# A linear-attention and MLP kernel whose five written-out queues are ordered anew with refitted transfer times

## The chip, the cores and the metric

One core of a Trainium2 chip runs one launch of the whole program. The metric is device time in microseconds (us), as the median of repeated runs. The engines are TensorE (PE, with its weight loads as PEld), VectorE (DVE), ScalarE (ACT), GpSimd (POOL) and SyncE (SP, whose queue issues the transfers).

## The reference

The input is a block of 2048 rows of 512 numbers. Two layers A and B follow each other, and both are applied twice with the same weights.

```python
def _A_ref(x, wqkv, w_phi, wo):
    q, k, v = ((x @ wqkv).reshape(B, S, 3, H, Dh)...)        # H = 32, Dh = 16
    phi_q = concat([softmax(q @ w_phi), softmax(-(q @ w_phi))])  # per head; the same for k
    kv, z = phi_k^T v, sum(phi_k)                            # over all 2048 rows
    o = (phi_q kv) / (phi_q z + 1e-6)
    return o.reshape(B, S, D) @ wo

def _B_ref(x, w1, w2):
    return relu(x @ w1) @ w2                                 # 512 -> 1792 -> 512

x = A_x
x = x + _A_ref(layernorm(x), A_wqkv, A_w_phi, A_wo)
x = x + _B_ref(layernorm(x), B_w1, B_w2)
x = x + _A_ref(layernorm(x), A_wqkv, A_w_phi, A_wo)
x = x + _B_ref(layernorm(x), B_w1, B_w2)
```

## The kernel before

The rows are worked on in 16 chunks of 128, and the MLP in 8 groups of 256. Each f32 operand of a product is held as the sum of two f16 numbers, high and low, and three products (high by high, high by low, low by high) stand for one. ACT makes most high parts by copying, and POOL or DVE subtract to get the low parts.

*Layer A.* Each chunk `x` is normalised (`n_a`), turned by a transposing DMA or at the start by PE (`xT`), and projected to `pk`, `pv` and `pq`. The feature map makes exponentials (`e_k`, `e_q`), a factor (`fm_k`, `fm_q`) and the products `p_k`, `p_q`. A product with `minus` gives the low part of `v` from the same bank after ACT has copied the high part (line 795). `kv` and `kvn` collect phi_k^T v over the rows, `pn` multiplies them with the transposed `pT`; a division gives `o`, which is split in high and low parts (`n_o`), turned to `oT` and projected by `pw`. `qs` is the copy of `pq` that goes to memory (`q_dram`) and comes back as `ql`. `xt_dram` keeps a chunk's `xT` for the later query projection.

*Layer B.* `n_b` is turned to `yT`. For most groups the hidden product (lines 1391 to 1500, `hidden_by_seven`) multiplies by seven half-size products in place of eight. It needs sums of weight blocks, made at the start by POOL and ACT (`sums`, `sums_h`, `sums_l`), kept in `s_dram`, and loaded again as `s` for each step (`fetch_sums`, line 1391, 512 KB into one of three buffers). ACT copies the intermediate results to `sn` (line 1446), and DVE adds them back (lines 1452, 1457). The output product by seven is line 1608, the plain one line 1549.

*The order.* Nothing runs in program order of this file. Each operation is registered with `add(engine, work, ...)` in a `Plan`: 4681 tasks, 1513 on PE, 972 on DVE, 1071 on ACT, 618 on POOL and 506 on SP. `ORDER` holds one string for each of the five queues. Read from left to right, a digit says how many of the tasks left over in this engine's list are skipped before the next is taken (`Z` adds 61). So the strings alone fix what each engine does after what. `order()` then replays the queues with the planner's model times and hands out the tasks by their modelled starts; with the queues fixed, its times decide only in which sequence the instructions of different engines are written down. `landing()` is the model's price of a transfer: time from issue to landing, and the time the queue takes for each. A transposing transfer is `turn`; a task with `work > 1.5` that isn't `turn` is another class, and all the rest the third. The issue itself is priced in `add`, for a transposing load in `transposed`: 1.3 us below 512 KB, else 1.85. [...]

The engines take their queues strictly in sequence. A step that stands too early makes everything behind it in its queue wait.

The function that the diff touches is `Plan.landing` (line 177), called by `Plan.order`, beside the table `ORDER`.

Of the kernel before, what the change touches and what calls it, by code (L numbers as in the profile page):

```python
# [54 lines left out]
DIGITS = "0123456789abcdefghijklmnopqrstuvwxyzABCDEFGHIJKLMNOPQRSTUVWXYZ"  # L55
ORDER = {
    PE:
        "000033222242210032000770204413339122603847310830209001180032710013140020331403160D516201xx12v04314031012"
        "555520eeee10cc0bbn0aaaaiiaaaa01070605600302011190011040000a058000200500344070101405046103050332700150055"
        "71783070351544403300111133311000004700000000000000000007090000d00b00f00i00j00000000000000000000001111133"  # L60
        "33333333304444444410222333133302222222222000000001112222201001106009000000000300090001111122000000000002"
        "222220110001030000000000000007090g000d00h000j0l00000j000000000000000000000000222222222111333333333334445"
        "55550444444444444445556666666607706666770605566677788888aaa099900700550446605550444444033333312222222222"
        "22222222222222201122201110110000000000011111444444444447777777060555555088880777770055999900700040001111"
        "111060000006b000000000000000001111111111010ps0r202000liij00g00e0ddeedd0c0f10dff0cdcc00a00807700904444445"
        "540330011311003330223307770667700aa0027005556605aaaaaaaaaaaaaaaaaaabbbccccccccdddee0000a0990807005514033"
        "30222011111111110400500000j000000g0000000000e000000000j0000000000000A0C0000000000000000000C000C000000000"
        "000000v000000000000000000000000l00000000000000000y000y000000000000000000z000000000000q0000000r0000000000"
        "0000000o00000000000000000000000v0000000000000000000000c000s000s0000000000000000000000e00000000000000e000"
        "0000000000v00w00000000000000000y000000v000000000000r000000000000000000000000h000000000000000000000000000"  # L70
        "00000000000000000000000000000000000000000000000000000000000000000000000000000000000000000000000000000000"
        "000000000000000000000000000000000000000000000000000000010",
    DVE:
        "330430210000e222011036000020dd0302203a35d33b602f230c100e0YdX0g00Te04f4Oe4g660Id5f004403902h20f1h1g10000e"
        "j0idg7063f04033028k222222220441312110343llm34j33h33333c320122121006k01i410200abe0q0d7n004100o03mf02j0400"
        "01800d4100003630136051150664650514099317011300aa108000131321521300060240661666058408070450020051411c3b32"
        "924302002063522322001113110223302004410209107025e01c12a2010203132152131811050718817569189841004090016011"
        "10211130226176625582756827360c00aahh0g000220b11107011063341509544225452332403000252031403514180701194406"
        "680881065160146002211062520331601410h4g0001232117011060045141010000000330520120000010k0100g00000b0a09102"
        "0c1b4002000030g3f311cx016u15s111003t3s032p6252LL4090HO80M706JZaZa05Z825467053513077Z4ZC1300Z00Zw044V1Zr7"  # L80
        "0201e120Zs21Zq10800d0ZjZP1ZO10912100ZG115501315041020de1001Zv102h3Zqg0004g422200292Zb00224002520303f2200"
        "22a002300024222817029200224007262110g2g2200201j02h3015022220b0228102a59010622002200211023100522220020102"
        "20021102000201023000342320022002000221022000010011010",
    ACT:
        "31201104220030005c5ba099fm088c306053cc10jj2902md2cj1003mZq320j141Zj0m2kZf0j1500k3k0j26gn2m5j1136312k3Mj4"
        "1222ll4010m10130h3021102301cc041gg310002801cc002060201bj2216312c1110k8jjd80g0f69da080d7c460307010aaa0301"
        "c0b0fa020c650400d40309gg18020b03600080740200100020850033494104501011403a3480262303201110141023500820a053"
        "032000020431012057115c53022201131020220251131303231010350243242021010142832204b4590302533333343350030004"
        "182b716191071018111222015261553544512362605599909808807cc0ccf00ef0ie00f0e2420a1d10b709250968073433a39383"
        "393570250a1912100510383067096106608533504321003044239a003305200550002041700122100605210643021004033020g0"  # L90
        "0e010524010504008d0770999051f05300322030014255016ecb101990u80607p067605v56060ep583m406I05G950D70Q677Zp6M"
        "6ZmL7777Zh805608043Zo44ZY032Zj04Zh4ZQ400011011040ZEf302ZQ52ZO4036311ZZjf33ZE110302224000ZZ31005042300030"
        "32200l605520052033135100f3ZG30141022010Ze22Zs0115044011102330006055246004030004140332501027011302B001044"
        "00014140220160j501360240306021g4021100222103020105042370501302070024400524401004003320030220030220030201"
        "03022103302040302200303321403020130220403305103000000",
    POOL:
        "10002540570095006800960A0z96019600607005908a00809e00710c91118100101106252201b01f4e8000044403005201ck20a1"
        "c10ac09fbb910000143032131201100000022e017215100071630221111162100200103022010304444300131323101110001111"
        "104470082466053022110046004200312201413444430003400000001ccc1300077b706686056051433300130220302222200022"
        "4050002200000100000000302104030000066000001000000aa010002d00009cc0k0juYua01U8100203W10Zo0T1000Zid203Zn30"  # L100
        "23322b01Zd100011105Zw000061000010g3302021302221d11044012201T5111Y101121000242010222141121441730200003000"
        "l13110002222a0022111d1114133001114070004411002422002221110044440333312100000000000002333220110000000100",
    SP:
        "200010100214060809Badf119eg02s8127nc5e065Cd1223322235b90a1220704i1g1jg112e31b3002708d0fe30e21e00g2q51na2"
        "D3320e11g013100A8f002573b3b4537580c42a4120171159565a6hb4aa358l6124133884t486Bc3fh77055454b9597255520w0c7"
        "73272a6067ac8cq5a46371644418136371259d052c10aa112b3a448a0902bcJb72946772692556651823o124907731w5314300r1"
        "p2668o4841367436D1qd3110d235h0moqw7011009d1v0g709a00ex2E40g06K4811b12807aHg8Q9la70826Q2Z15233k72721456j1"
        "535Q51430205h51043044504d122200403063529244302218504070226452432205040044440330113022110010",
}


# [32 lines left out]
class Plan:  # L144
# [1936 lines left out]
```

## Time and profile before

| what | value |
|---|---|
| median of 3 runs | 964.04 us (963.81 to 964.42) |
| profiled execution | 963.83 us, span 962.1 us |
| PE busy | 947.4 us, 98% |
| DVE, ACT, POOL busy | 694.8, 573.6, 647.5 us |
| memory traffic | 144 GB/s over the span, read 108.30 MB, written 30.15 MB |
| granted clock of PE | top tenth in all 40 slices |

Busy time is what an engine's instructions take in the profile; the ends of products on PE are modelled, so a busy PE isn't always at its peak. A wait is put down to the engine or transfer that released it last. The profile comes from one execution, and the span is 1.73 us shorter than that execution's device time.

### The profile page before, as it was taken

The numbers are of one execution on the slowest core, as the hardware profiler recorded it, in microseconds if no ns is written. First come the engines' busy times: TensorE is split into PE (matmuls) and PEld (weight loads), VectorE is DVE, ScalarE is ACT, GpSimd is POOL, SyncE is SP. The second block draws the span as 40 slices with busy tenths as digits, with TensorE's granted clock in tenths as the row PEclk, the third lists the DMA queues.
The fourth block names the chain that finished last, engine by engine and source line by source line (L and its number), as shares of the span: only waits on it lengthen the run. The fifth ranks groups of instructions, "written<-read, shape, count | busy, mean of one in ns | idle before, by whom it ended". The sixth has DMA issues, their size and how long they took to land.

```text
span 962.1 us, 23668 instructions
## 1 busy us (share of the span) xinstructions
PE 947.4 (98%) x9372; PEld 659.7 (69%) x9372; DVE 694.8 (72%) x1408; ACT 573.6 (60%) x1121; POOL 647.5 (67%) x634
## 2 busy tenths in 40 slices
PE   8999999999999999999999999999999999999997
PEld 5544555666665766566677775566666889888997
DVE  6899978856876877766566678987886575665455
ACT  7999978654554636454375555465555565555553
POOL 2699877778685857555376647267578888777644
PEclk9999999999999999999999999999999999999999
DMA  9387858499869697788649864599999786886541
GB/s 334 90 223 197 194 157 224 95 197 217 206 156 233 164 268 158 175 224 214 155 155 253 254 189 112 199 248 228 222 221 252 184 186 170 188 169 172 134 139 66
DMA packets 251807, 183.38 MB, mean 191 GB/s; under 512 B 180656, under 2 KB 188080, under 8 KB 251696
## 3 DMA queue, kind: packets, MB, share of 16 engines
q1 hardware_dynamic: 251696, 181.87, 74.3%
q8 instruction: 73, 1.20, 0.5%
q14 instruction: 38, 0.31, 0.1%
HBM read 108.30 MB, written 30.15 MB: 144 GB/s over the span
## 4 chain that ended last, share of the span: by engine, by line
PE 91%; DMA 2%; ACT 2%; POOL 2%; DVE 1%; issue 1%; SPq 0%; DVEq 0%; POOLq 0%; ACTq 0%
PE ph L1433 23%; PE py L1549 14%; PE py L1608 12%; PE pw L650 8%; PE pk L650 8%; PE pv L650 8%; PE pq L650 8%; PE ph L1513 3%; PE pn L1019 2%; PE kv L816 1%; DMA s<-s_dram 1%; DMA st_k<-in_A_wqkv_dram 1%; DMA wk_h<-n_u 1%; POOL sums L1289 0%; POOL p_q L734 0%
## 5 line engine op out<-in xcount | busy, mean ns | idle before, releaser
L1549 PE MATMUL py<-w,h 128*128 128x512 f16 x690 | 174.2, 379 | 0.0
L1433 PEld LDWEIGHTS <-s 128*128 128x128 f16 x2352 | 151.3, 98 | 28.3 <-DMA s<-s_dram 2.2
L1446 ACT ACTIVATE sn<-ph 128x128 f32<-128x128 f32 x294 | 80.6, 274 | 146.3 <-PE ph L1433 143.2
L650 PEld LDWEIGHTS <-xT 128*128 128x128 f16 x900 | 86.8, 98 | 99.1 <-DMA xT<-n_a 1.4
L1433 PEld LDWEIGHTS <-w 128*128 128x128 f16 x1764 | 111.0, 98 | 15.0 <-DMA wk_h<-n_u 1.4
L1433 PE MATMUL ph<-yT,s 128*128 128x128 f16 x1176 | 97.6, 219 | 1.1 <-DVE ph L1452 1.1
L1433 PE MATMUL ph<-yT,w 128*128 128x128 f16 x1176 | 97.6, 219 | 0.0
L1452 DVE TENSOR_TENSOR ph<-ph,sn 128x128 f32<-128x128 f32 x98 | 29.3, 299 | 92.3 <-PE ph L1433 48.5
L1549 PEld LDWEIGHTS <-h 128*128 128x128 f16 x690 | 61.4, 98 | 49.2
L734 POOL TENSOR_TENSOR p_q<-e_q,p_q 128x1024 f16<-128x1024 f32 x32 | 71.4, 2230 | 21.0 <-ACT p_q L730 21.0
L723 POOL TENSOR_TENSOR e_q<-e_q,fm_q 128x1024 f32<-128x1024 f32 x32 | 62.5, 1957 | 33.8 <-ACT fm_q L719 33.5
L734 POOL TENSOR_TENSOR p_k<-e_k,p_k 128x1024 f16<-128x1024 f32 x30 | 68.7, 2288 | 20.6 <-ACT p_k L730 20.5
L650 PE MATMUL pw<-wo_h,oT 128*128 128x512 f16 x256 | 81.4, 379 | 0.2 <-ACT qs L886 0.2
L650 PE MATMUL pk<-wk_h,xT 128*128 128x512 f16 x256 | 81.3, 379 | 0.0
L650 PE MATMUL pv<-wv_h,xT 128*128 128x512 f16 x256 | 81.2, 379 | 0.0
L723 POOL TENSOR_TENSOR e_k<-e_k,fm_k 128x1024 f32<-128x1024 f32 x30 | 59.5, 1983 | 28.7 <-ACT fm_k L719 27.7
L650 PEld LDWEIGHTS <-oT 128*128 128x128 f16 x384 | 37.0, 98 | 41.4 <-issue 1.0
L1457 DVE TENSOR_TENSOR ph<-ph,sn 128x256 f32<-128x256 f32 x98 | 41.9, 427 | 31.1 <-PE ph L1433 30.6
L1608 PEld LDWEIGHTS <-h 128*128 128x128 f16 x648 | 59.1, 98 | 6.4
L1229 POOL TENSOR_TENSOR w<-r 128x256 f32<-128x256 f32 x41 | 31.4, 766 | 40.0 <-ACT r L1225 40.0
L650 PE MATMUL pq<-wq_h,xq 128*128 128x512 f16 x168 | 56.6, 379 | 0.1
L1608 PE MATMUL py<-w,h 128*128 128x256 f16 x324 | 53.0, 273 | 0.0
(279 smaller groups left out, 2419.4 us busy)
## 6 DMA issues: line engine op xcount, KB each, us to landing
s<-s_dram SPq DMA_DIRECT2D x98, 512.0 KB, 4.4
q_dram<-qs SPq DMA_DIRECT2D x28, 256.0 KB, 3.8
ql<-q_dram SPq DMA_DIRECT2D x28, 256.0 KB, 3.7
u<-t_dram SPq DMA_DIRECT2D x13, 512.0 KB, 4.5
xt_dram<-xT SPq DMA_DIRECT2D x21, 256.0 KB, 4.2
xq<-xt_dram SPq DMA_DIRECT2D x21, 256.0 KB, 3.9
xe<-in_A_x_dram SPq DMA_DIRECT2D x16, 256.0 KB, 4.4
x<-in_A_x_dram SPq DMA_DIRECT2D x16, 256.0 KB, 4.2
```

The lines of the kernel that those rows point to most:

```text
L650: nc.tensor.matmul(pm.ap, xT.ap[:, a, k, :], W.ap[b][:, k, :], start=(k == 0 and i == 0), stop=(k == KC - 1 and i == 2))
L723: (nc.vector if fast else nc.gpsimd).tensor_tensor(e3, e3, sm.unsqueeze(2).to_broadcast([P, 2 * n, DH]), op=ALU.mult)
L734: (nc.vector if fast else nc.gpsimd).tensor_sub(part16(1, cols), part16(1, cols, ef), part16(0, cols))
L1019: nc.tensor.matmul(at()[:, g, :], pT.ap[:, a, 4 * i + g, :], r[b].ap[:, 4 * i + g, :], start=(j == 0), stop=(j == 2))
L1229: nc.gpsimd.tensor_sub(rf.ap[:, :2, :], r.ap.rearrange("p (a b) -> p a b", a=4)[:, ::3, :], block(1).unsqueeze(1).to_broadcast([P, 2, P]))
L1433: nc.tensor.matmul(at(r), weight_of(i, b, kk, s, summed), rows_of(y, i, a, kk), start=(first and kk == 0 and n == 0), stop=(kk == 1 and n ...
L1446: nc.scalar.activation(saved(i), at(2), AF.Copy)
L1452: add(DVE, 0.27, lambda: nc.vector.tensor_tensor(at(3), at(1), saved(2), op=ALU.add), reads=[(ph, 1), (sn, 2)], writes=[(ph, 3)], boost=10 ...
L1457: add(DVE, 0.40, lambda: nc.vector.tensor_tensor(wide(ph), wide(ph), wide(sn), op=ALU.add), reads=[(sn, 0), (sn, 1)], writes=[(ph, 0), (ph ...
L1513: nc.tensor.matmul(at()[:, j, cs.start * P:cs.stop * P], W1.at(b, k, slice(f * P, (f + 1) * P)), yT.ap[:, cs, a, k, :], stop=(k == KC - 1 ...
L1549: nc.tensor.matmul(py.ap, h[a].ap.rearrange("p j t -> p (j t)")[:, cols], W2.at(b, fs[j], slice(0, D)), start=(begins and j == k == 0), st ...
L1608: nc.tensor.matmul(py.ap[:, 256 * r:256 * r + 256], left[a], right[b], start=(s == 0 and r == 0 and k == 0), stop=(last and k == 2), skip_ ...
```

## The change

The strings of all five queues are replaced, and the three prices in `landing` are changed. No operation is added or removed, and no buffer changes its size or number. In numbers for common sizes: a 256 KB transfer 2.62 us before and 2.91 after; a 512 KB one 3.65 and 4.03; a transposing load of 256 KB 3.16 and 3.11, of 512 KB 4.33 and 4.61. Decoded, 845 of PE's 1513 tasks keep their place; on DVE 366 of 972, on ACT 361 of 1071, on POOL 253 of 618 and on SP 74 of 506. The mean shift is 0.88 places on PE, 1.32 on DVE, 1.40 on ACT, 1.20 on POOL and 3.90 on SP; the longest are 34 places on PE, 30 on DVE, 38 on ACT, 12 on POOL and 66 on SP. Some of the moves: the square of `st_q` on ACT from place 20 to 17; the `pv` product with `minus` on PE near 127 us from 102 to 111; `pn` products near 732 us from 1026 to 1033 and from 1030 to 1041; a `pw` near 830 us from 1244 to 1235; an `n_o` on ACT from 890 to 873 and a high `p_q` from 907 to 869; two stores to `xt_dram` near 432 us on SP from 246 to 208 and from 241 to 261.

The first line of each string, before and after, and the prices:

```diff
--- before.py
+++ after.py
     PE:
-        "000033222242210032000770204413339122603847310830209001180032710013140020331403160D516201xx12v04314031012"
...
+        "000032222422210032000770204413339122053847300840209002910032701013140304015041710D51620y1xx3040152030036"
...
     DVE:
-        "330430210000e222011036000020dd0302203a35d33b602f230c100e0YdX0g00Te04f4Oe4g660Id5f004403902h20f1h1g10000e"
...
+        "33043302100f3331221812211001di03b022c2022c42290112c1bg1Z110Y0hc00Te0g44e4Mg660Id500d440a302h20f1h1g100g0"
...
     ACT:
-        "31201104220030005c5ba099fm088c306053cc10jj2902md2cj1003mZq320j141Zj0m2kZf0j1500k3k0j26gn2m5j1136312k3Mj4"
...
+        "31011004220001105bb5aa09nf2087b0h1553cl0029h30dl2kc1003Zr30kk214Zk00l2Zgk3j6204k0k0ji722mm511U7331m23kb1"
...
     POOL:
-        "10002540570095006800960A0z96019600607005908a00809e00710c91118100101106252201b01f4e8000044403005201ck20a1"
...
+        "11030854006058009600960A09y6019600607060908a00809e007109b11181001011062522d010a1e94800910405340030c0fb11"
...
     SP:
-        "200010100214060809Badf119eg02s8127nc5e065Cd1223322235b90a1220704i1g1jg112e31b3002708d0fe30e21e00g2q51na2"
...
+        "200010002004069d020d8yea39920s07863014M556923482371b3b6b23m20070131g41g41410830c78f0k03fe0220eit2r101030"
...
@@ -177,10 +177,10 @@
     def landing(self, t):
 
         if t.turn:
-            return 2.0 + t.kb / 220, t.kb / 230
+            return 1.6 + t.kb / 170, t.kb / 193
         if t.work > 1.5:
-            return 4.8, 2.4
-        return 1.6 + t.kb / 250, t.kb / 385
+            return 4.4, 2.5
+        return 1.8 + t.kb / 230, t.kb / 306
 
     def add(self, engine, work, fn, reads=(), writes=(), makes=(), lock=False, kb=0, turn=False, boost=0,
             after=(), slack=None):
```

## Rows read from the trace of the kernel before

**Rows 1.** The page: busy time by engine; granted clock of TensorE in 40 slices.

```profile
PE 947.4 (98%) x9372; PEld 659.7 (69%) x9372; DVE 694.8 (72%) x1408; ACT 573.6 (60%) x1121; POOL 647.5 (67%) x634
...
PEclk9999999999999999999999999999999999999999
```

**Rows 2.** Stretches: length, busy PE PEld DVE ACT POOL, clock, DMA share, GB/s.

```profile
0.00:30.00 30.00, 25.45 (x161) 18.37 (x162) 21.19 (x56) 22.89 (x37) 8.28 (x24) 1.00 0.80 290
...
930.00:960.00 30.00, 27.16 (x333) 24.52 (x330) 16.77 (x32) 12.20 (x30) 14.21 (x21) 1.00 0.19 66
...
sum 962.10, PE 947.41 PEld 659.70 DVE 694.81 ACT 573.58 POOL 647.46; mean PE 28.71 PEld 19.99 DVE 21.05 ACT 17.38 POOL 19.62
```

**Rows 3.** Waits of PE: total us, times, longest us.

```profile
PE wt_k L1731 <- DMA st_k<-in_A_wqkv_dram: 2.0, 2, 1.5
PE ph L1433 <- DMA s<-s_dram: 1.9, 2, 1.2
```

**Rows 4.** Timeline of PE, single lines: start us, us, line, operation, idle before.

```profile
23.11 1.04 PE L1731 MATMUL wt_q<-ident,st_q 128*128 128x128 f32 x8
...
127.83 0.39 PE L795 MATMUL pv<-v,minus 128*128 128x512 f16 x1 [0.69 <-ACT v L791]
...
189.91 0.38 PE L650 MATMUL pw<-wo_h,oT 128*128 128x512 f16 x1 [0.25 <-ACT qs L886]
190.12 0.38 PE L650 MATMUL pw<-wo_l,oT 128*128 128x512 f16 x1
...
385.84 0.84 PE L1433 MATMUL ph<-wq_h,s 128*128 128x128 f16 x12 [0.73 <-DMA s<-s_dram]
...
438.09 0.84 PE L1433 MATMUL ph<-wq_l,s 128*128 128x128 f16 x12 [1.18 <-DMA s<-s_dram]
...
732.07 0.51 PE L1433 MATMUL ph<-wk_h,w 128*128 128x128 f16 x6 [1.26 <-DMA wk_h<-n_u]
...
834.70 0.38 PE L650 MATMUL pw<-wo_h,oT 128*128 128x512 f16 x1
```

**Rows 5.** Timeline of ACT, single lines.

```profile
21.22 0.58 ACT L1736 COPY wT_q<-wt_q 128x512 f32<-128x512 f32 x1
21.68 1.92 ACT L387 ACTIVATE wq_l<-st_q 128x2048 bf16<-128x2048 f32 x1
...
127.18 0.60 ACT L791 ACTIVATE v<-pv 128x512 f16<-128x512 f32 x1
...
188.22 1.15 ACT L1279 ACTIVATE sums_h<-sums,s_w 128x1024 f16<-128x1024 f32 x1 [3.18 <-POOL sums L1289]
...
827.11 0.63 ACT L564 ACTIVATE n_o<-o 128x512 f16<-128x512 f32 x1 [1.34 <-issue]
...
832.25 0.28 ACT L1446 ACTIVATE sn<-ph 128x128 f32<-128x128 f32 x1 [0.34 <-PE ph L1433]
```

**Rows 6.** Timeline of SP's queue, single lines.

```profile
378.05 3.27 SPq L578 DMA_TRANSPOSE pT<-p_q  x1
...
432.08 0.46 SPq L772 DMA_DIRECT2D xt_dram<-xT  x1
...
721.96 3.74 SPq L578 DMA_TRANSPOSE pT<-p_q  x1
...
829.00 1.24 SPq L578 DMA_TRANSPOSE oT<-n_o  x1
```

**Rows 7.** Pieces of the chain that ended last: start us, us, what.

```profile
381.41 4.38 DMA s<-s_dram
431.67 6.37 DMA s<-s_dram
...
726.42 5.60 DMA wk_h<-n_u
```

**Rows 8.** DMA issues: transfer, times, KB, median us from issue to landing.

```profile
s<-s_dram SPq DMA_DIRECT2D x98, 512.0 KB, 4.4
...
oT<-n_o SPq DMA_TRANSPOSE x28, 3.7
```

More of the change, by code (lines that the diff above doesn't have):

```diff
@@ L68 @@
[L68 to L70 removed]
+        "000032222422210032000770204413339122053847300840209002910032701013140304015041710D51620y1xx3040152030036"
+        "6663g0f0e1d0ccc0bn0aaaaiiaaaa00170605600302011190201040000a050709302002020120520030441541500230101450605"
@@ new lines @@
+        "16160153505503122010000002201100000020002000000000000000058000d00bh00k00l0000000000000000e00000000111112"
+        "22222222224444403330222333444002222222220100000001112201110330800b00000000050000002000003001000000000020"
+        "11111000000140000000000000000060006000bbh0000i0000h00000000000900000000000000222222222011302222222222333"
+        "44444444033333333333444555550033304444445555566677788880799908006660550446660555504030222222222201111111"
+        "111111110000000000011111101100001111112201114444444444477777005555555504888077777777b0099900700100201111"
@@ new lines @@
+        "11100500900000900000000000000011111111100000ooq20011ljk0j00g000ddffdd00bbf10ggd0ecdc01099007700084464444"
+        "033350021111044030223307770660660a00882005556660aaaaaaaaaaaaaaaaaaabbbccccccccdddeee03c00099999080005504"
+        "4030222011111111110200300000000eh000000000000d000000000i00000H0000000D000000000000000000000000000v000000"
+        "0r00x000000000000000000000000n00000000000000000A0C000000000000000G0I000000000000000000000000000p00000000"
+        "00000000n0000000000000000000000000s000s00000000000A0000z00000000000000000000000000h00000000n0000000000H0"
@@ new lines @@
+        "20c1b4030000030g3f12100a6u0t50r00040t30r3q325N2M03aJ30O88M070ZbJZa0064Z60001313222Z6771120Z0ZxZ01Zv14030"
+        "Zq6h0520eZt10Zr200000Zl01bb1ZM202110ZG16150ZB47161013fg101n10l1102Zq3Zp01052320102Ze28006224006252002f2f"
+        "2002200i2301304332810218170252070l2520i022p210201j02307610222c0b30000b6292106220022102210230005222010221"
+        "0221022102210220023000442221022002200221022000010013100",
+    ACT:
+        "31011004220001105bb5aa09nf2087b0h1553cl0029h30dl2kc1003Zr30kk214Zk00l2Zgk3j6204k0k0ji722mm511U7331m23kb1"
+        "32630kk1310110i4h2021410301ccj013g10501300dd600200201c2j31742142b110kk8jd07g0f69da0807cc460027010aaa03e2"
+        "200af8f37105040e00302180e2604a09000380405200252070070403494840652005103a3483025302220100140303500d106053"
+        "03010002503001208146156a553312210300220155050503402004034043240121110514226214b4048336450333340622030020"
+        "38c2005003305201708020111060244233223062610448880778800c6b00aeae0e0d00ee2d42220d88b17931790847545b4a0383"
+        "39357062b320171162b5a10932205777090533533021141044019290833922015100200304520211060520043032110404302000"
+        "e07c1024010044008d070a6990510e5300322102014255016eb0290909u870807o076055u60s603d47m8K840Ha0507CR0677NZo7"
+        "MZm6707660Zf4554460Zo40Zm23ZV204ZhZR4130340120i003ZD3ZS360244ZMk2324401114ZB13ZZa312400ZZ421161042221043"
+        "022n070304406020337420500e320Zm4002Zy20Zw102211004420250103Ze320m700524060244000141032224190211410220441"
+        "022204103p310710550163044m071315040014002000302250040322013032200630440600413005100332003022040302510302"
+        "000220140022041022014040325103020400201400225103000000",
```

54 lines of the change are left out of this document (16 added, 38 removed).

## The prediction

> **What bounds the kernel now.** I read the page's engine table first: TensorE (PE) is busy 947.41 us of the 962.1 us span, no other engine over 694.8, and its clock stays in the top tenth in every slice [rows 1]. Since no multiplication is added or taken away, the change can only move the 14.69 us in which PE is not busy, and the next view was therefore busy time by stretches of 30 us [rows 2]: 4.55 us of it is missing before 30.00, 2.84 between 930 and 960, 2.10 behind 960. That leaves 14.69 − 9.49 = 5.20 us for the 900 us in the middle. The last two are the end of the program, whose last products wait for nothing that can be ordered otherwise. So the question is how much of 5.20 us goes, what happens to the 4.55 us at the head, and whether new pauses come.
>
> PE's waits and its timeline then name the pauses [rows 3, 4]. Five are in the middle: 0.69 us before 127.83 (ScalarE's `v`), 0.25 before 189.91 (ScalarE's `qs`), 0.73 before 385.84 and 1.18 before 438.09 (both a load of `s`), 1.26 before 732.07 (the transposing load of `wk_h`). They sum to 4.11 of the 5.20; the rest is in pieces of 0.5 us and less. A pause is some 0.16 us longer than shown, as two 512-column products start 0.21 us apart but are drawn 0.38 us long (189.91 and 190.12 [rows 4]); with that they are 0.85, 0.41, 0.89, 1.34 and 1.42. At the head PE waits 2.0 us for `st_k` [rows 3].
>
> **How the change acts.** The five queues are written-out lists and nothing in them is an operation more or less. Decoding both sets of lists gives, by place in its queue, how far a step moves: PE 0.88 places in the mean, VectorE (DVE) 1.32, ScalarE (ACT) 1.40, GpSimd (POOL) 1.20, SyncE (SP, which issues every transfer) 3.90; 845 of PE's 1513 steps keep their place exactly. The new constants reach the chip only through these lists. So I costed the known pauses one by one, then what was moved far.
>
> **Head (4.55 us idle).** PE's order is nearly the old one; the loads of `st_k`, which end two of its waits, keep their places. ACT's square of the 1 MB `st_q` (1.92 us [rows 5]) goes three places forward, ahead of two `wT_q` copies and one `xT` copy. The last of the three ended at 21.22 + 0.58 = 21.80; 1.9 us later it ends at 23.7, and PE reaches the block of `wt_q` that uses its bank at 23.11 [rows 4, 5], so 0.6 us may be lost there, and nothing behind gives it back. Against this, the square no longer stands behind the copies, so that ACT's exponentials come when they came. A second exchange puts the short square of `phi` before that of the second half of `st_k`, which lies on the way to the first `pf_k`. I take +0.4; bounds −0.3 (the rows that PE transposes at 20 us come a little earlier) and +2.0 (the whole square lands on PE).
>
> **127.83 (0.69 shown, 0.85 true).** PE's product with `minus` waits for ACT's `v`, which ran at 127.18 [rows 5]. The product goes nine places later on PE (102 to 111), ACT's step five later. That pause goes, but 140 to 190 us has pauses and near-pauses on ACT and POOL which take part of a shift back: `sums_h` at 188.22 waits 3.18 us for POOL [rows 5]. I take −0.5; bounds −0.85 and 0.
>
> **189.91 (0.25 shown, 0.41 true).** `qs` stood behind `sums_h` on ACT, which waited for POOL's sums until 188.22 [rows 5]. POOL makes these sums five and six places earlier, ACT the `sums_h` six earlier. −0.3; bounds −0.41, and +1.15 if `sums_h`, 1.15 us long, is still ahead of something that PE wants.
>
> **385.84 (0.89 true).** The `s` was issued at 381.41, directly behind a transposing load that held SP for 3.27 us from 378.05, and landed 4.38 us later [rows 6, 7]. In the new SP list the same two stand in the same sequence. Only a product of 0.22 us that stood ahead of the wait (`kvn`) goes ten places forward, and the chain that makes the transposed tile comes a little earlier. −0.2; bounds −0.89 and +0.3.
>
> **438.09 (1.34 true).** `s` took from 431.67 to 438.04, 6.37 us, where the median is 4.4 [rows 7, 8]. Right behind it the old list has a store of `xt_dram`, issued at 432.08 [rows 6], which moves beside it. The new list takes that store, and a second one near it, to other places, and puts a `kv` product of 0.6 us just ahead of the product that frees the buffer, so the issue may be later by as much. −0.4; bounds −1.34 and 0.
>
> By the Trainium skill, "DMA: Bandwidth & Descriptors", section "Anatomy of one DMA — SWDGE (gpsimd) path", a transfer takes about 2.0 us and its bytes at 436 GB/s, which for this one is an estimate of 3.2 us. The page fits another issuing path; by it the old 3.65 us of the planner was the nearer, the new 4.03 goes the wrong way, and the terms at 385.84 and 438.09 would be nothing: 0.6 us more than my sum. The rows speak against it: the median of 98 is 4.4 us [rows 8].
>
> **732.07 (1.42 true).** `wk_h` was issued at 726.42, behind a transposing load that held SP for 3.74 us from 721.96, and took 5.60 us [rows 6, 7]. The new list has the same steps in the same sequence there. Two `pn` products of 0.33 us go from before the wait to behind it; the pause gets longer and the time behind it shorter. 0; bounds −1.42 (it lands in time) and +0.7.
>
> **Moved far.** Around 830 the `pw` products (834.70 [rows 4]) stand nine places earlier, and their `oT` is transposed from an `n_o` made at 827.11 on ACT [rows 5] and issued at 829.00 [rows 6]. A median landing of such a load, 3.7 us [rows 8], gives 832.7 in the old order. ACT's `n_o` is 17 places earlier in the new one, but PE would reach the `pw` at about 830.7. I take +0.3; bounds 0 and 1.5. The other moved PE steps have no pause in the old order, and I can't price each; I take 0, with −0.9 (the small pauses of 5.20 − 4.11) and +3 as bounds, the upper from the 3.18 us that one ACT step here stood blocked [rows 5].
>
> **Sum.** 0.4 − 0.5 − 0.3 − 0.2 − 0.4 + 0 + 0.3 + 0 = −0.7 us. The profiled execution took 963.83 (span 962.1 and 1.73 around it): 963.13. That execution is 0.21 under the median of 964.04, whose runs reach 963.81, so I leave the forecast at 963.2.
>
> **Rivals.**
>
> 1. *The fit works.* If all `s` loads and the transposed weight are issued as early as they are needed, 0.89 + 1.34 + 1.42 go, and with 0.85 and 0.41 in the first part 4.91 us: 963.83 − 4.91 + 0.4 = 959.3; with only two of three transfers in time about 960.7. For it: the planner's old price for `s` (3.65 us) is below the measured 4.4, so in the old order it was taken to arrive earlier than it does. Against: in two of the three places the list is the same there, and what holds SP is a transposing load for 3.3 to 3.7 us, which the planner's tasks count as 1.85 us, a number that isn't changed.
>
> 2. *ACT is blocked in its order (the other side).* ACT's high half of a `p_q` goes from place 907 to 869 and an `n_o` from 890 to 873, near 800 to 835. At 1121 ACT instructions in the span [rows 1], 35 in 30 us, that is some 33 and 15 us earlier. Each needs a chain across PE, DVE and POOL that must come as much earlier. ACT takes its queue in order; if the operand is late, the `sn` copies behind (0.28 us, as at 832.25 [rows 5]) wait, PE's next product into that bank needs them, and PE stops. It decides from the point where an operand is later than the free time ahead of such copies, 0.34 us at that one. A wait like the 3.18 us of `sums_h`, less 0.34, costs 2.8 us: 963.83 + 2.8 = 966.6; two of them, 969.4. For it: no other steps of ACT have moved as far. Against: none of the five large pauses of the old order was ended by an `sn`, so the copies have had room.
>
> 3. *It does not do what it says.* The constants price transfers, and the places where PE pauses hang on the SP hold and on ACT; new and old are two draws of one planner. Then what goes in one place comes in another: 963.8 ± 0.5.
>
> **Chances.** Forecast 0.38 (961.5 to 965.5), rival 1 0.27, rival 2 0.21, rival 3 0.14. 0.2% is 1.93 us, about what a measurement of this kernel can tell from no change: faster is below 962.1, slower above 966.0. Faster: 0.27 and a sixth of the forecast's, 0.33; slower: 0.21 and 0.01 of the tails, 0.22; the rest, 0.45, the same. For 8 in 10 the range reaches to rival 1 and to the single wait of rival 2: 959.3 to 967.0. The forecast's own range is 961.5 to 965.5.
>
> **What would show it.** In PE's waits of the changed kernel: `v` gone; `qs` gone; `s` still there once or twice, with a sum of about 1.3 us instead of 1.9; `wk_h` still at 1.2 or more; `st_k` at 2.0. In the table by stretches: 25.0 to 25.4 in the first 30 us; 720 to 750 still over 1.2 us short of 30. If all of 360 to 450 and 720 to 750 reads 30.00, rival 1 holds. If a new wait of over 1.5 us for ACT or DVE stands between 780 and 860 and ACT shows a step with idle time ended by POOL ahead of it, rival 2 holds. The prediction is wrong in kind if the head changes by over 1 us or if PE's busy time itself does.

## The result and the profile after

The changed kernel takes 966.51 us (median of 22 runs, 964.39 to 971.88), the kernel before 964.28 beside it (22 runs, 962.57 to 967.71): a ratio of 1.0024, 95% interval 1.0015 to 1.0033. It is slower by 2.2 us, small but beyond the measurement. The forecast was 963.2, faster or the same, with 961.5 to 965.5 as its own range. The sign is wrong. That the time lies inside the wide range (959.3 to 967.0) is luck: the range reached so far up for a single long wait near 800 to 835 (rival 2), and no such wait came.

The profiled execution of the changed kernel took 965.55 us, its span is 963.8. The page, first the engines and the clock, then the chain that ended last:

```profile
PE 948.3 (98%) x9372; PEld 658.6 (68%) x9372; DVE 698.1 (72%) x1408; ACT 570.3 (59%) x1121; POOL 645.4 (67%) x634
...
PEclk9999999999999999999999999999999999999999
...
PE 83%; DMA 5%; DVE 4%; POOL 4%; ACT 3%; issue 1%; SPq 0%; DVEq 0%; POOLq 0%; ACTq 0%
```

The same line of the kernel before:

```profile
PE 91%; DMA 2%; ACT 2%; POOL 2%; DVE 1%; issue 1%; SPq 0%; DVEq 0%; POOLq 0%; ACTq 0%
```

PE has the same 9372 products at the same clock as in [rows 1]. Its busy time is 0.9 us larger since each pause hides up to 0.16 us behind the drawn end of a product. So the extra time is pauses. The chain points the same way: 17% of it runs outside PE, where it was 9%. The stretches of the changed kernel, columns as in [rows 2]:

```profile
0.00:30.00 30.00, 26.07 (x166) 18.49 (x167) 22.58 (x62) 23.78 (x39) 9.10 (x25) 1.00 0.86 317
...
240.00:270.00 30.00, 29.14 (x202) 17.47 (x200) 25.55 (x37) 16.34 (x25) 22.01 (x17) 1.00 0.76 190
...
390.00:420.00 30.00, 29.18 (x247) 17.26 (x245) 22.56 (x47) 14.16 (x27) 16.59 (x17) 1.00 0.81 180
420.00:450.00 30.00, 29.13 (x335) 20.80 (x334) 17.96 (x33) 15.42 (x36) 18.48 (x17) 1.00 0.80 192
...
660.00:690.00 30.00, 28.09 (x285) 17.95 (x283) 21.77 (x39) 15.05 (x33) 19.11 (x14) 1.00 1.02 200
...
720.00:750.00 30.00, 30.00 (x343) 21.58 (x341) 19.57 (x45) 17.08 (x41) 25.07 (x25) 1.00 1.00 227
```

The stretch from 720 to 750 is full, so the pause for `wk_h` is gone. Three stretches lose 0.8 to 0.9 us, and one, 660 to 690, loses 1.9. PE's waits, against [rows 3]:

```profile
PE ph L1433 <- ACT sn L1446: 2.3, 3, 0.9
PE wt_k L1731 <- DMA st_k<-in_A_wqkv_dram: 1.5, 2, 1.0
PE pq L650 <- DMA xq<-xt_dram: 1.3, 1, 1.3
...
PE ph L1433 <- DVE h L1164: 0.9, 1, 0.9
...
PE ph L1433 <- DMA s<-s_dram: 0.6, 2, 0.4
```

`v`, `qs` and `wk_h` have left this list. What came is ScalarE's `sn` three times (before 395.0, 437.1 and 662.6), a `pq` that waits for `xq` (673.6) and an `h` of VectorE (266.1).

I count a pause from start to start: the distance between two products less the usual one for the first (0.22 us for 512 columns, 0.06 for 128). Summed over the program this is 15.6 us before and 17.5 after. Less by 5.5 are the head (1.0), 190 (0.4), 386 (0.5), 438 for `s` (1.3), 675 (0.4), 732 (1.4) and 826 (0.5). New are 1.02 at 266, 0.98 at 395, 1.03 at 437, 0.61 at 509, 0.74 at 662, 1.48 at 673, 0.8 near 753, and 0.3 each at 105 and 342, in all 7.3; what is left is in smaller pieces.

**The place that costs most, read step by step.** SP's queue, first in the kernel before, then in the changed one:

```profile
655.09 0.53 SPq L892 DMA_DIRECT2D q_dram<-qs  x1
655.71 2.46 SPq L1391 DMA_DIRECT2D s<-s_dram  x2
```

```profile
653.30 0.38 SPq L1391 DMA_DIRECT2D s<-s_dram  x1
653.77 0.45 SPq L997 DMA_DIRECT2D ql<-q_dram  x1
654.31 0.38 SPq L1391 DMA_DIRECT2D s<-s_dram  x1
654.79 0.42 SPq L892 DMA_DIRECT2D q_dram<-qs  x1
...
665.53 2.96 SPq L578 DMA_TRANSPOSE pT<-p_q  x1
668.76 0.36 SPq L877 DMA_DIRECT2D xq<-xt_dram  x1
```

The store of `qs` keeps its place on SP, 359 in both lists. What changed is what goes out just ahead of it: in the new list an `s`, a `ql` and another `s`, all in the 1.5 us before it. (The first of these `s` stood ahead of the store in the old list too, but it was issued at 642.65 and had landed at 649.18.) The store goes out 0.3 us earlier than before and lands 4.2 us later. The chain of the changed kernel in this stretch (start, us, what) shows the price:

```profile
654.79 6.83 DMA q_dram<-qs
...
661.73 0.64 ACT n_b L564
...
668.76 4.78 DMA xq<-xt_dram
...
673.59 0.82 PE pq L650 x3
```

The store takes 6.83 us, where it took 2.4 before. ScalarE's high copy of `n_b` stands for it (it waits for a buffer that this store reads), with `sn` behind it in the queue, and PE behind `sn`. ScalarE's timeline, then PE's:

```profile
661.73 0.63 ACT L564 ACTIVATE n_b<-xn_b 128x512 f16<-128x512 f32 x1 [1.55 <-DMA q_dram<-qs]
662.26 0.43 ACT L1446 ACTIVATE sn<-ph 128x128 f32<-128x128 f32 x2
```

```profile
662.57 0.49 PE L1433 MATMUL ph<-wk_h,w 128*128 128x128 f16 x6 [0.58 <-ACT sn L1446]
...
673.59 0.39 PE L650 MATMUL pq<-wq_h,xq 128*128 128x512 f16 x1 [1.32 <-DMA xq<-xt_dram]
```

The `n_b` copy and `sn` have exactly the same places on ScalarE in both lists (690 and 691). What was moved are loads ahead of the transfer that one of them waits for.

**The same thing near 395.** The changed kernel issues a transposing load of `yT` at 388.77, behind the second `pT`; before, it was issued at 383.24 and landed 3.7 us later. Now it takes 5.54. SP's queue of the changed kernel, then its chain:

```profile
385.71 2.97 SPq L578 DMA_TRANSPOSE pT<-p_q  x1
388.77 1.26 SPq L578 DMA_TRANSPOSE yT<-n_b  x1
```

```profile
388.77 5.54 DMA yT<-n_b
...
394.33 0.03 ACT n_u L564
...
394.66 0.27 ACT sn L1446
...
394.97 0.49 PE ph L1433 x6
```

The `n_u` copy (place 407 in both lists) wants the buffer that `yT` is read from, `sn` (408) stands behind it, and PE behind that. At 437 a `yT` issued at 431.02 took 5.34 us, with the same end; but there ScalarE's own list moved too: the `n_u` copy stood behind two `sn` (place 449) and now stands ahead of them (447). The prices in `landing` give such a load (256 KB) 3.11 us, down from 3.16, and the store 2.91.

**266 is another case.** No transfer is in its chain. The new list puts an `fm_q` and a high `p_k` on ScalarE ahead of the relu (`h`) that PE needs. The first waits for VectorE until 263.16, the second for GpSimd until 263.80, and the relu, which ran at 261.04 in the kernel before, runs at 264.76. Here it is ScalarE's own order that holds up PE.

### The profile page after: what moved, and what is told of

Same layout as the page of the kernel before. It is cut to its first block, busy times and chain, and to the rows that moved or that the text cites. A ratio compares the mean times of both kernels' runs of the same rounds, so it can differ in the third digit from the quotient of the medians.

```text
span 963.8 us, 23636 instructions
## 1 busy us (share of the span) xinstructions
PE 948.3 (98%) x9372; PEld 658.6 (68%) x9372; DVE 698.1 (72%) x1408; ACT 570.3 (59%) x1121; POOL 645.4 (67%) x634
## 4 chain that ended last, share of the span: by engine, by line
PE 83%; DMA 5%; DVE 4%; POOL 4%; ACT 3%; issue 1%; SPq 0%; DVEq 0%; POOLq 0%; ACTq 0%
PE ph L1433 21%; PE py L1608 12%; PE py L1549 12%; PE pw L650 8%; PE pq L650 8%; PE pk L650 7%; PE pv L650 7%; PE ph L1513 3%; PE pn L1019 2%; DMA s<-s_dram 2%; DMA yT<-n_b 1%; POOL e_k L723 1%; POOL p_k L734 1%; PE kv L816 1%; DMA q_dram<-qs 1%
## 5 line engine op out<-in xcount | busy, mean ns | idle before, releaser
L1433 PEld LDWEIGHTS <-w 128*128 128x128 f16 x1764 | 110.9, 98 | 17.5 <-issue 2.8
L734 POOL TENSOR_TENSOR p_q<-e_q,p_q 128x1024 f16<-128x1024 f32 x32 | 69.4, 2170 | 23.6 <-ACT p_q L730 20.7
```

Of the source, the lines that this page charges most:

```text
L734: (nc.vector if fast else nc.gpsimd).tensor_sub(part16(1, cols), part16(1, cols, ef), part16(0, cols))
L1433: nc.tensor.matmul(at(r), weight_of(i, b, kk, s, summed), rows_of(y, i, a, kk), start=(first and kk == 0 and n == 0), stop=(kk == 1 and n ...
```

## The experiments

My theory A: the loss sits in single places of the new lists, where a transfer that frees a buffer is issued behind others, lands late, and stops ScalarE, which works in order, with steps of PE's behind (at 266 without the transfer). Rivals: B, a pause that is removed comes back further on; C, the prices or the lists act as a whole; others are named where they come. Each kernel was timed against the kernel before on the same chip; the ratios are to that. A ratio whose interval holds 1 can't be told from no change.

**Which pauses belong to the lists.** The old lists with the new prices, and the changed kernel again:

```diff
 ORDER = old lists
-    return 2.0 + t.kb / 220, t.kb / 230
+    return 1.6 + t.kb / 170, t.kb / 193        # and the other two
```

> The kernel before with the three new prices alone; all five lists are the old ones. Theory A (the time is in the lists): 964.0, within 0.1% of before, the pauses of PE at 127.8, 385.8, 438.1 and 732.1 stay, their idle in the middle 5.2 us +- 0.5. Rival C (the prices act by themselves, through the sequence in which instructions of different engines are written down and so through the semaphores): up to 2.3 us slower, as the changed kernel, with pauses that before doesn't have.

Ratio 0.9992 (0.9981 to 1.0002). The prices by themselves make no difference that can be told. But its trace, of the same lists as before, was of use: the pauses for `v` (0.85), `qs` (0.41) and `wk_h` (1.46) are there again; the one for `s` before 386 has 0.39 in place of 0.89, and the one before 438 is not there at all. In their place stands one of 1.6 at 105 for `xT`, which wasn't in the first trace.

> The changed kernel itself again, for a second trace. If the pauses before 266, 395, 437, 662 and 673 us are made by the lists, each is there again with 0.5 us or more; if they were drawn by one execution's landing times, some are gone and others of the size stand elsewhere. 966.0 to 966.8 either way.

Ratio 1.0034 (1.0021 to 1.0046). All five are there again: 1.01 at 266, 0.87 at 395, 0.79 at 437, 0.70 at 662, 1.24 at 673; so is the one at 509 (0.53). Those near 753 are 0.29 and 0.20 now, and one of 0.49 for an `oT` at 826 is new. The changed kernel's second trace, PE's waits:

```profile
PE ph L1433 <- ACT sn L1446: 1.9, 3, 0.7
...
PE pq L650 <- DMA xq<-xt_dram: 1.1, 1, 1.1
...
PE ph L1433 <- DVE h L1164: 0.8, 1, 0.8
```

So there are two sorts of pauses. Those of the first sort come in both traces of the changed kernel, and in no trace of the old lists that has no edit at the place; they belong to the lists. The others are drawn anew by the landing times of each execution. In us of PE not busy (length less busy, from the stretches of each trace; a dash where that kernel's own edit lies in the stretch):

| trace | 0 to 30 | 235 to 460 | 630 to 700 | 700 to 750 |
|---|---|---|---|---|
| before | 4.55 | 1.91 | 0.32 | 1.26 |
| old lists, new prices | 3.66 | 0.74 | 0.58 | 1.30 |
| one load exchanged at the head (below) | – | 0.68 | 0.74 | 0.96 |
| one store moved near 655 (below) | 4.69 | 1.00 | – | 1.68 |
| one chain moved near 385 (below) | 4.29 | – | 0.48 | 1.26 |
| old lists up to 700 us (below) | 3.34 | 0.47 | 0.29 | – |
| changed | 3.93 | 2.85 | 1.94 | 0.00 |
| changed, again | 3.67 | 2.44 | 1.74 | 0.13 |

From 235 to 460 the trace on which the prediction rested has the largest number of the old lists in this table. Single traces overlap all the same: in the kernels below that join pieces of both lists, this stretch has 0.47 to 2.53 us not busy with the old lists in it and 1.89 to 2.88 with the new.

**Repairs in the changed kernel.** First ScalarE's places:

```diff
 ACT, near 394 us                      near 437 us                  near 264 us
-n_u high (407)                       -n_u high (447)              +relu h (266)
 sn (408)                              sn, sn, ups (448 to 450)     ups fm_q (264)
+n_u high                             +n_u high                     p_k high (265)
                                                                   -relu h
```

> The changed kernel with six places of ScalarE's list put back: two high copies of n_u (near 394 and 437 us) behind the sn copies that PE waits for, one relu (near 265 us) ahead of a p_k copy. Theory A (ScalarE stands in its queue for a buffer that a transfer frees late, and PE behind it): PE's pauses before 266.1 (1.02), 395.0 (0.98) and 437.1 (1.04) go, 3.0 us in all; the one at 437 may come back in part as a wait for s, so -2.0 to -3.0 us, 963.5 to 964.5. Rival B (a pause that goes comes back further on, as PE arrives earlier at the next thing that is late): under 1 us gained, new pauses within 30 us of each place. The pauses before 662.6 and 673.6 stay under both.

Three steps are moved. Near 437 and 264 this is the old sequence again; near 394 neither list has it so. Ratio 1.0012 (1.0001 to 1.0024), about half of the loss. In its trace the three pauses are 0.23, nothing, and 0.31 (for an `sn`, at 442): the stretch from 390 to 420 is full. ScalarE still stands for `yT`, but with nothing behind it that PE wants soon:

```profile
392.98 0.28 ACT L1446 ACTIVATE sn<-ph 128x128 f32<-128x128 f32 x1
394.33 0.42 ACT L564 ACTIVATE n_u<-xn_b 128x256 f16<-128x256 f32 x1 [1.07 <-DMA yT<-n_b]
```

That one execution had other pauses: 4.6 us of 630 to 700 were not busy in it, where the changed kernel has 1.9 (1.08 for an `oT` at 645, and 1.89 and 2.01 at the two known places). No edit here explains that, and it took 967.87 where the median of the kernel is 965.2. For rival B the three places speak clearly against, the time less so.

> The changed kernel with one store to q_dram (near 655 us) issued three places earlier on SP, ahead of two loads of s and one of ql. Theory A: the store lands about 4 us earlier (657.5 and not 661.6), ScalarE's n_b copy no longer stands for it, PE's pause before 662.6 (0.74, sn) goes, and with it the pause before 673.6 (1.48, xq), since the n_u that ends SP's wait ahead of the load comes some 2 us earlier: -2.2 us, 964.3. Rival B: only the 0.74 goes, the xq load is late by itself behind the x and pT transfers: -0.7 us or nothing, 965.8 to 966.5.

```diff
 SP, near 653 us
+q_dram<-qs (359)
 s<-s_dram (356), ql<-q_dram (357), s<-s_dram (358)
-q_dram<-qs (359)
```

Ratio 1.0010 (0.9999 to 1.0022). The store takes 2.8 us, and the pause before 662 is gone, as both say; the one before 673 is 0.83 in place of 1.48. The median, 964.35, is theory A's, but the second pause is gone only in part.

> The changed kernel with both edits together, seven moved steps. Theory A: the sum, -4.2 to -5.2 us against the changed kernel, 961.3 to 962.3, below the kernel before by 2 us. Rival B: 964.5 to 966, no gain against before.

Ratio 1.0002 (0.9990 to 1.0015): four moved steps (three on ScalarE, one on SP; the expectation counts seven) take back what the change lost, 0.22% by the difference of the ratios. The changed kernel was not timed beside it. That is 2 us, not the 4.2 to 5.2 forecast. The sum fell short since the wait for `xq` stayed (1.76). There rival B was right: `n_u` comes earlier, but `xq`, issued at 665.35, was 5.3 us under way behind `x` and `pT`. So I moved those.

```diff
 SP, near 656 us
+pT<-p_q (364)
 yT<-n_b (360), s (361), yT<-n_b (362)
-x<-x_dram (363)
-pT<-p_q (364)
 xq<-xt_dram (365), wk_l (366), s, s, wk_l, xq, ql (367 to 371)
+x<-x_dram
```

> The kernel with both edits, and two more moves on SP: a transposing load of pT (near 662 us) back ahead of the yT load, where the kernel before has it, and a load of x (near 661 us) behind the loads of xq and s. Theory A (a load lands when what was issued ahead of it has landed; xq was 5.3 us under way behind x, pT and s): xq lands 2.5 to 3.5 us after its issue, PE's pause before it (1.76 in the kernel with both edits) goes under 0.5, -1.3 to -1.8 us against both edits, 961.8 to 962.3. Rival B (the wait goes elsewhere): 963.0 to 963.8, with a new pause for an oT, s or ql between 640 and 690.

A miss: 1.0024 (1.0014 to 1.0033), as slow as the changed kernel. `xq` does land 2.8 us after its issue, but SP's queue shows what the move broke, and PE's waits the price:

```profile
655.84 5.21 SPq L578 DMA_TRANSPOSE pT<-p_q  x1
661.15 1.26 SPq L578 DMA_TRANSPOSE yT<-n_b  x1
...
669.46 0.34 SPq L877 DMA_DIRECT2D xq<-xt_dram  x1
```

```profile
PE ph L1433 <- ACT sn L1446: 2.5, 1, 2.5
```

A transposing load of 512 KB holds SP's queue for 5.21 us behind two loads of `s`, where the planner counts 1.85. The two `yT` behind it are issued late. ScalarE's `n_u` stands 2.74 us for the second of them, and `sn` and PE stand behind it:

```profile
668.27 0.42 ACT L564 ACTIVATE n_u<-xn_b 128x256 f16<-128x256 f32 x1 [2.74 <-DMA yT<-n_b]
```

The same mechanism, made by my own hand. A second price comes on top: behind this pause of 2.65 us the granted clock of PE was 0.50 (1.2 GHz of 2.4) for 3.4 us, from 671.2 to 674.6, and products of 512 columns started 0.43 us apart in place of 0.22. By these numbers that is an estimated 1.7 us.

**One step alone, in the kernel before.**

```diff
 SP, near 655 us
-q_dram<-qs (359)
 s<-s_dram (360)
+q_dram<-qs
```

> The kernel before with one exchange on SP near 655 us: the store to q_dram behind the load of s that follows it, nothing else. Theory A (a store lands when the loads issued ahead of it have landed; a ScalarE copy stands for its buffer): the store lands near 661.5 in place of 657.5, ScalarE's n_b copy starts 2 us later than its data is there (659.1), PE pauses 1 to 1.7 us before 662 and, as xq comes 2 us later, up to 1.5 before 673: +1.0 to +2.5 us, 965.0 to 966.5. Rival D (it needs the whole window of new order; a single store has room): no pause of PE before 662, 963.5 to 964.3.

Ratio 1.0008 (0.9999 to 1.0017), not told from no change, and less than forecast. The trace shows why. The store takes 4.89 us where it took 2.4, and ScalarE stands for it 1.15 us, but PE only 0.35 (0.18 shown). One load ahead of the store uses up the room, the three of the changed kernel exceed it. The chain, ScalarE and PE of this kernel:

```profile
655.29 4.89 DMA q_dram<-qs
```

```profile
660.29 0.63 ACT L564 ACTIVATE n_b<-xn_b 128x512 f16<-128x512 f32 x1 [1.15 <-DMA q_dram<-qs]
```

```profile
661.13 0.49 PE L1433 MATMUL ph<-wk_h,w 128*128 128x128 f16 x6 [0.18 <-ACT sn L1446]
```

> The kernel before with one chain of three steps moved as the new lists have it: the high copy of n_b on ScalarE (393), its low part on GpSimd (216) and the transposing load of yT on SP (212) go behind the step that the new list has ahead of each, so that yT is issued behind the second pT near 385 us. Theory A: yT lands near 394 in place of 387, the next n_u copy on ScalarE stands for its buffer, the sn copy behind it is late, PE pauses 0.8 to 1.1 us before 395: 964.4 to 965.2, +0.1%. Rival: the n_u copy has room (it ran at 393.2 with its buffer free at 387), no pause of PE, 963.5 to 964.3.

```diff
 ACT  -n_b high (393)   POOL -n_b low (216)    SP  -yT<-n_b (212)
       ... five steps          ... four steps       s, pT<-p_q (213, 214)
      +n_b high               +n_b low             +yT<-n_b
```

Ratio 1.0012 (1.0001 to 1.0023), by the median 1.2 us. The time is what theory A forecast, but not for its reason. `yT` is issued at 391.17 and lands 3.07 us later, and the profile shows nobody who waits for it; `n_u` runs at 394.32 directly behind the step ahead of it. PE does pause 0.77 before 394, where the first two traces of the old lists have no such wait, but for an `sn` that stands ahead of `n_u`. What held that up is GpSimd, where the moved low part of `n_b` now runs ahead of a short step of `stat_a`:

```profile
389.98 1.16 POOL L567 TENSOR_TENSOR n_b<-xn_b,n_b 128x512 f16<-128x512 f32 x1
391.10 0.55 POOL L630 TENSOR_TENSOR stat_a<-stat_a,nhalf 128x1 f32<-128x1 f32 x1
```

ScalarE waits for what becomes of it, with `sn` three steps behind:

```profile
391.93 0.81 ACT L627 ACTIVATE xn_a<-x,stat_a 128x512 f32<-128x512 f32 x1 [2.19 <-DVE stat_a L632]
```

In the kernel before, the `stat_a` step ran at 389.80 and ScalarE's `xn_a` at 390.84. Another 0.95 us before 396 is for an `oT` that SP issues behind this `yT`, at 393.12 and not at 389.59. So a step moved in one in-order queue does cost PE here, but this run is no evidence for the late landing at 395. That rests on the two traces of the changed kernel and on the repair.

**The lists by stretches.** Dependences run forward in time, so lists can be spliced: all steps that began before a cut in the profile of before in one sequence, those behind in the other. All of these kernels have the new prices.

```diff
-ORDER = old lists
+ORDER = old before 235 us, new from 235 to 460, old behind     # win_a
+ORDER = old before 630 us, new from 630 to 700, old behind     # win_b
+ORDER = old before 235 us, new from 235 to 700, old behind     # mid_new
+ORDER = new before 235 us, old from 235 to 700, new behind     # mid_old, mid_old2
+ORDER = old before 700 us, new behind                          # late_new
+ORDER = new, but old from 630 to 700 us                        # hole_b
```

> The lists of before, with the new lists for the steps that began between 235 and 460 us in its profile. Theory A (the loss sits in single places of the new lists): ScalarE is late before 266, 395 and 437 us for n_u and p_k copies, 3.0 us of PE pauses, against 0.5 to 1.5 us of the s pauses of before that differ from one execution to the next: +1.5 to +2.5 us, 965.0 to 966.0. If the lists only hurt as a whole: no pause there, 963.5 to 964.3.

Ratio 1.0008 (0.9994 to 1.0021): less than forecast, and not told from no change. The three pauses are there, smaller (0.61, 0.44, 0.76).

> The lists of before, with the new lists between 630 and 700 us. Theory A: the store of q_dram lands behind two loads of s, ScalarE's n_b copy stands for it, xq lands late behind x and pT: pauses before 662 and 673 us of 2 to 3 us together, +1.5 to +2.3 us, 965.0 to 965.8. If not: 963.5 to 964.3.

Ratio 1.0055 (1.0039 to 1.0071): three times the forecast. The store takes 7.4 us, and the pauses before 662 and 673 are 1.6 and 2.0; but there is also 1.4 for an `oT` at 646, and behind the seam at 700 there are 1.1, 0.4 and 0.4, none of which the traces of the old and of the new lists have. (A 1.3 for `wk_h` at 739 is the old lists' own.)

> The lists of before up to 235 us and from 700 us, the new lists between; the complement of the kernel that was 0.05% under before. Theory A: it carries the whole loss and none of the gains, +2.4 to +3.4 us against before, 966.0 to 967.0, at least as slow as the changed kernel. If the lists act as a whole: about half of the changed kernel's loss, 965.

Ratio 1.0071 (1.0053 to 1.0089). It carries the whole loss, but also a pause of 3.26 at 717, behind the seam, and around it 3.4 us at a granted clock of 0.50. (A 1.8 at 743 is for `wk_h`, as in the old lists.) So a splice from new to old near 700 us costs something itself, and the sizes of these two don't measure the new lists alone.

> The lists of before with the new lists between 630 and 700 us, and in it the store to q_dram moved four places forward on SP, ahead of the two loads of s and the one of ql. Theory A: most of the 5.3 us that this window costs hangs on the store: PE's pause before 662 (1.6) goes, xq and the steps behind come 2 to 3 us earlier, 965.5 to 967.5. Rival D: the pauses for oT (645), xq (673), h (713) stay, 0.5 to 1.6 us less, 968.3 to 969.5.

```diff
 SP, in win_b, near 655 us
+q_dram<-qs
 s<-s_dram, ql<-q_dram, s<-s_dram
-q_dram<-qs
```

The store moves three places, not four. Ratio 1.0054 (1.0035 to 1.0072), no better than win_b. The `sn` pause before 662 is gone as forecast (0.91 for an `s` is there), and so is the one for `xq`; but 1.94 at 713 came, with a granted clock of 0.50 for 3.4 us soon behind it. Rival D holds for the time: with the seam there, the time doesn't hang on the store.

> The new lists, with those of before between 630 and 700 us. Theory A: what the changed kernel loses in that window (2.2 us before 662 and 673) goes, the ScalarE pauses at 266, 395 and 437 stay: 963.8 to 965.0, 0.05 to 0.1% over before. Rival D: the loss is made in 235 to 460 as well or by the seams, 965.5 or more.

Ratio 1.0016 (1.0007 to 1.0026); the changed kernel beside it had 1.0034. The stretch from 630 to 700 is nearly full (69.88 of 70). About half of the loss is there, and half stays, with the pauses at 266 (1.01) and 437 (0.93) and a wait for `s` at 754 (1.77). The one at 395 is not in this trace, with the same lists there.

> New lists up to 235 us and from 700 us, the lists of before between. Theory A: as the one with new lists from 700 us, less 0.4 (the qs pause near 190 us) and 0 to 1.0 (the head): 961.3 to 962.6, faster than before by 0.15 to 0.25%, and the pauses before 265, 395, 437, 662 and 673 us are not there. Rival C: 963.5 to 965.

Ratio 0.9995 (0.9985 to 1.0004).

> The kernel with new lists up to 235 us and from 700 us and those of before between, again: it had 0.9995 (0.9985 to 1.0004). Theory A: 0.9985 to 1.0, under the kernel before by less than 0.15%; the changed kernel's loss against it, 0.29%, stays.

Ratio 0.9992 (0.9982 to 1.0003). Twice a little under the kernel before and never clearly. None of the five pauses is in its first trace; in its second a wait for `h` of 0.63 stands at 264, on the product that waits at 266 in the changed kernel. Against the changed kernel it has 0.3% less, so the loss lies between 235 and 700 us, as far as the seams allow.

> The lists of before for all steps that began before 700 us in its profile, the new lists for those behind. Theory A: what the new lists make better here stays (the pause of 1.4 us for wk_h at 732, two of 0.55 in all near 822 to 826), against one of about 0.6 for s near 753: -1.3 us against before, 962.5 to 963.0. Rival C (lists act as a whole, a part of them has no gain of its own): 964.0 or more.

Ratio 1.0008 (0.9999 to 1.0018). The pause for `wk_h` is gone, as are those near 822, but a wait of 1.1 for `oT` at 713, behind this splice's seam too, took their place.

**Two single loads.**

```diff
 SP, kernel before, at 3.8 us
-xe<-in_A_x_dram (6)
 st_q<-in_A_wqkv_dram (7)
+xe<-in_A_x_dram
```

> The kernel before with one exchange on SP: the third load of xe (256 KB, issued at 3.84 us) behind the load of st_q. If that load is why the second half of st_k landed at 8.62 us and not at 7.6 (it shares the transfer engines with it): it lands near 7.6, PE idles 1.0 us less in the first 30 us, 963.0 to 963.3. If the landing times at the head just differ from one execution to the next (the prices alone gave 7.2 with the old list): no difference that can be told, 963.6 to 964.4.

Ratio 1.0002 (0.9993 to 1.0010): no difference that can be told. The head differs between executions.

```diff
 SP, lists of before behind 235 us, near 728 us
 wk_h<-n_u (406)
-x<-x_dram (407), yT<-n_b (408), wq_l<-t_dram (409)
 s<-s_dram (410)
+yT<-n_b
 oT<-n_o (411)
+x<-x_dram, wq_l<-t_dram
```

> The new lists up to 235 us, the lists of before behind, with three moves on SP near 728 us: a load of yT, one of x and one of wq_l go behind the load of s (the last two also behind the oT load) that follow them. Theory A (a load that lands late does so for what shares the transfer engines with it, behind it too): wk_h lands 4 us and not 5.6 after its issue, PE's pause before 732 (1.4) goes; with the qs pause near 190 (0.4): -1.2 to -1.8 us against before. Rival E (wk_h waits for the transposing load ahead of it, and the order behind it doesn't matter): the pause stays, 0.4 us less, no difference that can be told.

Ratio 0.9991 (0.9982 to 1.0001). The pause stays (1.52), and the chain has the load as long under way as before:

```profile
726.47 5.69 DMA wk_h<-n_u
```

That looks like rival E, but the edit didn't make the condition. It put an `s`, twice the size, where the `x` was, 1.3 us behind the load, and left the `yT` where it was, 1.9 us behind it. SP's queue of this kernel:

```profile
727.76 0.54 SPq L1391 DMA_DIRECT2D s<-s_dram  x1
728.40 1.23 SPq L578 DMA_TRANSPOSE yT<-n_b  x1
```

In the changed kernel the load goes out at 727.79. The same two transfers stand ahead of it (`pT` and `s`), but behind it only this goes out in the next 5.5 us:

```profile
729.57 0.36 SPq L1391 DMA_DIRECT2D s<-s_dram  x1
```

In all ten traces with a `yT` 1.9 us behind the load, it takes 5.5 to 5.8 us; in the ten with only an `s` behind it, 3.9 to 4.1, or 2.6 to 3.0 where the `s` ahead was issued earlier as well. So the traces speak for theory A: what is issued behind `wk_h` goes with its late landing, and the new lists would have removed this pause by taking `x` and `yT` away from there. No run changes that alone, so it is not shown.

## Why the prediction was wrong

**The step that failed** is the term "The other moved PE steps have no pause in the old order, and I can't price each; I take 0". It was worth 1.02 + 0.98 + 1.03 + 0.61 + 0.74 + 1.48 + 0.8 + 0.6 − 0.4 = +6.9 us in this pair of traces. The bound of +3 that I gave it came from one blocked step; there were six places that both traces of the changed kernel show (266, 395, 437, 509, 662, 673), 5.9 us in the first and 5.1 in the second. I looked at PE's steps, which moved 0.88 places in the mean, where SP's moved 3.90: a step of ScalarE that keeps its place comes later when the transfer it waits for lands later (395, 662), and a move of two to four places on ScalarE itself is enough (266, 437). The repair of four steps gives back 0.22%, as much as the change lost, and clears 266, 395, 437 and 662. What the pauses at 509 and 753 are worth was only seen, not tested, and the one at 673 went only in kernels that lost the time elsewhere.

**The known pauses** gave 5.1 us (1.0 + 0.4 + 0.5 + 1.3 + 1.4 + 0.5), where my sum has 0.7. 2.8 of it was drawn, see below. `wk_h` (term 0) went, 1.4: I compared the steps ahead of the load, which are the same, and not those behind it. The place near 830 (term +0.3) gained 0.5, but has 0.49 for an `oT` in the second trace. 189.91 went, as forecast. 127.83 (term −0.5) gave nothing: the wait for `v` is gone, and a `kv` that waits for `p_k` (0.40), an `xT` (0.20) and smaller ones take its place, 1.33 us in that stretch both before and after.

**385.84 and 438.09** went for no reason of the change. Other traces of the same old lists show 0.39 and 0 there: one execution's landing times, priced as if the lists had made them. The head (term +0.4) is the same: 3.2 to 4.7 us idle with the old lists there (nine traces), 3.0 to 4.1 with the new (ten).

**Rival 2 named the mechanism**, a ScalarE step that stands for its operand with `sn` behind it, but at steps that ScalarE itself moved far, near 800 to 835; nothing happened there (780 to 840 is full). It happened where ScalarE's steps moved little or not at all: at 395 and 662 they kept their places and stood for buffers that transfers free, at 266 and 437 they moved two to four places. Rival 1 failed where the prices are: `yT`, priced at 3.11 us, took 5.54 and 5.34, the store, priced at 2.91, took 6.83. **Rival 3** was right that what goes in one place comes in another, not that the two are equal: 5.5 us went and 7.3 came. Of its signs, the prediction had `v` and `qs` right; `wk_h`, the full stretch from 720 to 750 and the 26.07 in the first 30 us came out against it.

The store's row shows that transfers of SP's queue land behind what was issued ahead of them: 2.4 us with none of the three loads just ahead, 4.89 with one, 6.83 and 7.4 with all. In each of the 20 traces all 527 transfers of this queue land in the order of their issue. By the Trainium skill, "DMA: Bandwidth & Descriptors", section "Two DMAs through the same engine are not ordered", the descriptors in one queue of a DMA engine start in order but are pipelined, and the page promises no order of completion. The trace agrees that they are pipelined: at 655 five transfers of the changed kernel were under way at once. It adds that here the landings kept the order, and the price.

## What to carry to other kernels

Where a written-out order moves transfers, follow each moved transfer to the buffer that it frees, to the in-order engine that waits for that buffer, and to what stands behind it there; an engine whose own list hardly changed is no cover. Look at what goes out just ahead of a transfer, and just behind it, even where its own place is the same. Take a second trace of the same kernel before pricing single pauses: those that come back belong to the program, the rest to that execution. When an experiment moves one transfer away, see what takes its place, and read in the trace whether the forecast came by the way that was forecast: the test near 728 us failed on the first, the one-chain kernel on the second. A repair that moves a transposing load forward should be read for how long it holds its queue, not only for when it lands.

## What was not expected of the hardware

The issue of a 512 KB transposing load held SP's queue for 2.97 us in one place and 5.21 in another, behind two loads of 512 KB. A store of 256 KB, the same one, took 2.4 to 7.4 us, by the loads ahead of it. All transfers of SP's queue landed in the order of issue, 527 of 527 in every trace. The landing times of the same lists differ between executions so far that a pause of 1.34 us was 0 in the next trace. And in the three profiled executions with a granted clock of 0.50 within the program, it came with one of PE's longest pauses (1.94, 2.65 and 3.26 us) and stayed for 3.4 us; pauses of 2.01 and 2.03 elsewhere had none, so the pause's length alone doesn't tell.
